# Second net last, with two sets of x buffers, and the stationary operand of the down products at the far end of the on-chip memory

## The chip, the cores and the metric

The kernel runs on one core of a Trainium2 chip. The metric is the time of one execution on the device in microseconds (us); the median of several runs counts. The core has TensorE (PE in the profile; its weight loads are PEld), VectorE (DVE), ScalarE (ACT), GpSimd (POOL) and SyncE (SP), whose queue issues all DMA transfers of this kernel. The on-chip memory has 128 partitions; sums of matmuls are made in PSUM banks and copied out by DVE or ACT.

## The reference

Three stages follow each other: an attention within chunks of 64 rows, a mixture of eight experts whose gate is normalised over rows and columns in turn, and a second net.

```python
attn = softmax(scale * q_c @ k_c.T)            # 4 batches x 8 heads x 9 chunks of 64, head_dim 64
x = (attn @ v_c) as [2304, 512]
P = exp(x @ w_gate - max)                      # [2304, 8]
for _ in range(8): P normalised by rows, then by columns
x1 = sum over e of P[:, e] * (relu(x @ w1[e]) @ w2[e])      # w1 [8, 512, 1024], w2 [8, 1024, 512]
h = max(x1 @ v1, x1 @ v2, x1 @ v3)             # the second net: [512, 768] each
out = h @ w_out                                # [768, 512]
```

The second net's weights come in as 64-bit numbers and are decoded on the chip.

## The kernel before

**Precision.** Each operand of a large product is split into a high and a low half (`hilo`, lines 180 to 182: ACT copies the high half, DVE or POOL subtracts to get the low one). A product is then three matmuls: high by high, high by low, low by high.

**Tiling.** The 2304 rows are 18 tiles of 128 in three blocks `sb` of six. Each block's x stands in the buffers `xh` and `xl`, in the seven combinations of Strassen's scheme (four quarters and their differences). There is one set of these buffers, so a new block's x has to be put where the old one stands.

**Items.** The list `phases` (line 86) says which block goes through which net: "M" is the experts (32 items, each a pair of 128 hidden features), "m" the second net (nine items: three pairs of features by three weight matrices). Before the change the order is M of block 0, M of 1, m of 0, M of 2, m of 1, m of 2; I call these phases M0, M1, m0, M2, m1, m2. An item runs `up(n)`: seven products of six matmuls of 384 columns (line 235), numbered pos 0 to 6. ACT copies the first three sums out (`s`, line 240), DVE adds the next (`c`, line 243), and `finish` makes the activations `hh` and `hl`. The down products of the item before (`down`, line 267: six tiles of six matmuls of 512 columns in an M item, spread over three items in m) stand between the products; `hh` and `hl` are their stationary operand. After a down tile DVE adds it to `acc` (line 290 or 299).

**Work between the products.** `at(n, pos, fn)` puts a function behind product `pos` of item `n`. Every engine executes its own list in that order, and so does SP's queue.

- `decode_all` (lines 410 to 447) decodes the second net's weights: 24 jobs of eight or nine steps. A job's first DVE instruction (line 388) writes the tile `scm`. It shares its one buffer (tag `dhi`) with the job's last result `dhi`, which is stored to the DRAM array `scr` at line 447. So the next job's first step waits for that store to land. In the kernel before, all steps lie in the 30 items after M1's first one, eight steps an item.
- `x_load` (four quarters in 12 transfers), `x_sums` (four differences on DVE) and `x_put` (per product one ACT copy and one subtraction on DVE or POOL) make the next block's x in the last four items before each phase; `x_put(pos)` writes over the x of product `pos` right after its last use.
- `y_out` transposes a finished tile of the experts' output and stores it in `ys`, in the items after an M phase.
- `fetch` and `fetch2` load an item's weights (`wh`, `wl`; `w2h`, `w2l`) from DRAM on SP's queue. Every third item's `wh` and `wl` stand in a third buffer, pool `late`, at the upper end of the memory.

Of the kernel before, what the change touches and what calls it, by code (L numbers as in the profile page):

```python
# [9 lines left out]
F32 = mybir.dt.float32  # L10
F32R = mybir.dt.float32r
# [7 lines left out]
P = 128  # L19
# [10 lines left out]
KD = DM // P  # L30
SB = 3
TS = NT // SB
W = TS * P // 2
NPAIR = E * F // 256
# [3 lines left out]
NPE = 6  # L38
# [9 lines left out]
def kernel(ctx: ExitStack, tc: tile.TileContext, qk, vv, wg, wts, wts2, out):  # L48
    nc = tc.nc
    pool = lambda name, bufs=1, **kw: ctx.enter_context(tc.tile_pool(name=name, bufs=bufs, **kw))  # L50
    cp = pool("const")
    wp = pool("w", 2)
    hp_ = pool("h", 2)
    tp_ = pool("t", 1)
    raws = ExitStack()
    rp = raws.enter_context(tc.tile_pool(name="raw", bufs=1, side="right"))
# [13 lines left out]
    mr = cp.tile([1, P], F32, name="mr")  # L70
    rs = cp.tile([P, NT], F32, name="rs")
    cs = cp.tile([P, E], F32, name="cs")
    cp.tile([P, 480], F32, name="gap")
    xh = cp.tile([P, 7, 2, W], F32R, name="xh")
    xl = cp.tile([P, 7, 2, W], F32R, name="xl")
    xs = dram.tile([NT, P, KD, P], F32, name="xs")
    ys = dram.tile([NT, P, KD, P], F32, name="ys")
# [5 lines left out]
    wts2 = wts2.bitcast(I32)  # L83


    phases = [("M", 0), ("M", 1), ("m", 0), ("M", 2), ("m", 1), ("m", 2)]
    items, first_of = [], []
    for kind, sb in phases:
        first_of.append(len(items))
# [11 lines left out]
    st, sw, wh, wl, w2h, w2l = {}, {}, {}, {}, {}, {}  # L101
# [85 lines left out]
    def up(n):  # L187
        it = items[n]
        bank = {"a": ps_a.tile([P, 512], F32, name="pa", tag="pa"),
                "g": ps_g.tile([P, 512], F32, name="pg", tag="pg"),  # L190
                "b": ps_b.tile([P, 512], F32, name="pb", tag="pb")}
        bank = {k: t[:, :W] for k, t in bank.items()}
        begun = set()
        tiny = lambda nm: tp_.tile([P, W], F32, name=nm, tag=nm)
        m2 = it["kind"] == "m"
        if not m2:
            c = tp_.tile([P, 3, W], F32, name="c", tag="c")
        elif it["i"] == 0:
            mt[0] = big[0].tile([P, 4, W], F32, name="m", tag="big")
            c = mt[0]  # L200
        else:
            c = tp_.tile([P, 3, W], F32, name="c", tag="c")
        if it["down"]:
            hh = hp_.tile([P, 4, W], F32R, name="hh", tag="hh")
            hl = hp_.tile([P, 4, W], F32R, name="hl", tag="hl")
            it["h"] = (hh, hl)

        def finish(q, src):

            if not m2:  # L210
                nc.scalar.activation(out=hh[:, q], in_=src, func=AF.Relu)  # L211
                if q.start == 0:
                    nc.scalar.activation(out=src, in_=src, func=AF.Relu)  # L213
                    nc.gpsimd.tensor_tensor(out=hl[:, q], in0=src, in1=hh[:, q].bitcast(F32),  # L214
                                            op=ALU.subtract)
                    return
                nc.vector.scalar_tensor_tensor(out=hl[:, q], in0=src, scalar=0.0,  # L217
                                               in1=hh[:, q].bitcast(F32), op0=ALU.max, op1=ALU.subtract)
                return
            m = mt[0]  # L220
            if it["i"] == 0:
                if q.start == 3:
                    nc.scalar.copy(out=m[:, q], in_=src)
                return
            nc.vector.tensor_tensor(out=m[:, q], in0=src, in1=m[:, q], op=ALU.max)
            if it["i"] == 2:
                hilo(hh[:, q], hl[:, q], m[:, q])

        s = {}
        for pos, (wi, xi, b) in enumerate(PRODUCTS):  # L230
            ps = bank[b]
            for k in range(2):
                ws = slice(k * P, (k + 1) * P)
                for i, (x, y) in enumerate(((wh[n], xh), (wh[n], xl), (wl[n], xh))):
                    nc.tensor.matmul(ps, lhsT=x[:, wi, ws], rhs=y[:, xi, k], start=b not in begun,  # L235
                                     stop=k == 1 and i == 2, skip_group_check=True)
                    begun.add(b)
            if pos < 3:
                s[pos] = tiny(f"s{pos}")
                nc.scalar.copy(out=s[pos], in_=ps)  # L240
            elif pos < 6:
                q, other = {3: (0, 0), 4: (1, 1), 5: (2, 2)}[pos]
                nc.vector.tensor_tensor(out=c[:, q], in0=ps, in1=s[other], op=ALU.add)  # L243
                if pos == 4:
                    finish(slice(0, 2), c[:, 0:2])
                elif pos == 5:
                    finish(slice(2, 3), c[:, 2:3])
            else:
                finish(slice(3, 4), ps.unsqueeze(1))
            yield pos  # L250
# [94 lines left out]
    def x_put(pos):  # L345
        i = PRODUCTS[pos][1]
        hilo(xh[:, i], xl[:, i], xst[i], nc.vector if pos % 2 == 0 else None)

    def x_head(j, r, eng):

        cols = slice(j * P, (j + 1) * P)
        T = ap_.tile([P, 4, 2, P], F32, name="xT", tag="xT", bufs=1)
        for o, a, b in ((T[:, 0], r[:, 1, 0:2], r[:, 0, 0:2]), (T[:, 1], r[:, 1, 2:4], T[:, 0]),
                        (T[:, 2], r[:, 1, 2:4], r[:, 1, 0:2]), (T[:, 3], r[:, 0, 2:4], T[:, 1])):
            eng.tensor_tensor(out=o, in0=a, in1=b, op=ALU.subtract)
        yield
        raw = r[:, 0].rearrange("p (i k) q -> p i k q", i=2)
        nc.scalar.copy(out=xh[:, 0:2, :, cols], in_=raw)
        nc.scalar.copy(out=xh[:, 2, :, cols], in_=r[:, 1, 2:4])
        nc.gpsimd.tensor_tensor(out=xl[:, 0:2, :, cols], in0=raw, in1=xh[:, 0:2, :, cols].bitcast(F32),  # L360
                                op=ALU.subtract)
        nc.gpsimd.tensor_tensor(out=xl[:, 2, :, cols], in0=r[:, 1, 2:4], in1=xh[:, 2, :, cols].bitcast(F32),
                                op=ALU.subtract)
        for i in range(2):
            c = slice(3 + 2 * i, 5 + 2 * i)
            nc.scalar.copy(out=xh[:, c, :, cols], in_=T[:, 2 * i:2 * i + 2])
        yield
        for i in range(2):
            c = slice(3 + 2 * i, 5 + 2 * i)
            nc.vector.tensor_tensor(out=xl[:, c, :, cols], in0=T[:, 2 * i:2 * i + 2],  # L370
                                    in1=xh[:, c, :, cols].bitcast(F32), op=ALU.subtract)
        yield


    big = [None]

    def decode_load(srcs):
        w = big[0].tile([P, 512, 2], I32, name="w64", tag="ld", bufs=3)
# [72 lines left out]
    ap_ = att.enter_context(tc.tile_pool(name="att", bufs=2))  # L451
    wones = ap_.tile([P, 2 * DM], BF16, name="wones", tag="eT", bufs=1)[:, 0:DM]
    q_t, v_t, s_t, e_t, et_t, at_t, raw_t = {}, {}, {}, {}, {}, {}, {}
# [152 lines left out]
    def at(n, pos, fn):  # L606
        bg.setdefault((n, pos), []).append(fn)

    for m in range(NT - NPE):
        t, n = NPE + m, 1 + m  # L610
# [8 lines left out]
    n = NT - NPE + 2  # L619
# [6 lines left out]

    def att_close():
        att.close()
        big[0] = pool("big")

    def raw_close():
        raws.close()
# [5 lines left out]
        for step in range(4):  # L638
            at(g + step // 3, (0, 1, 6, 1)[step], lambda g=g, step=step: keep(g, step))
    dec, folds = decode_all(), fold_all()  # L640
    for a in range(NPAIR + 1, first_of[2] - 1):
        for b in range(7):
            for _ in range(1 + (b == 3)):
                at(a, b, lambda: next(dec, None))
    at(first_of[2] - 2, 6, lambda: [None for _ in dec])
    f0 = 4 * NRAW + 2
    for i in range(NRAW * TS + 2):
        at(f0 + i // 4, (0, 2, 4, 5)[i % 4], lambda: next(folds, None))
    for k in range(1, len(phases)):
        n0 = first_of[k]  # L650
        g = x_load(k)
        for i in range(13):
            at(n0 - 4 + i // 7, i % 7, lambda g=g: next(g, None))
        for step in range(4):
            at(n0 - 2, step + 2, lambda step=step: x_sums(step))
        for pos in range(7):
            at(n0 - 1, pos, lambda pos=pos: x_put(pos))

    def warm(n):
        p = wk.tile([P, 512], F32, name="warm", tag="wk")  # L660
# [3 lines left out]
    with tc.manual_schedule():  # L664
# [14 lines left out]
        for k in range(NPE + 2):  # L679
            if k < NPE:  # L680
                att_qk(k)
                load_qk(k + 3)
            if k >= 2:
                att_pv(k - 2)
                load_v(k + 1)
            if 1 <= k <= NPE:
                att_norm(k - 1)
            if k < NPE:
                att_exp(k, 2)
            if 1 <= k <= NPE:  # L690
                att_T(k - 1)
            warm(4 if k < NPE else 0)
            if k == 0:
                prep(0, 0)
                raw1(1)
            if k == 1:
                prep(0, 1)
            if k == 3:
                prep(0, 2)
                raw2(1)  # L700
            if xg:
                next(xg.pop(0))
            if k >= 3 and k % 2:
                g = x_head(k // 2 - 1, raw_t[k // 2 - 1], nc.gpsimd if k < NPE else nc.vector)
                next(g)
                next(g)
                xg.append(g)
# [72 lines left out]
```

## Time and profile before

| | us |
|---|---|
| three runs | 1940.75, 1938.32, 1941.76 (median 1940.75) |
| the profiled execution | 1934.4 |
| its span, first to last instruction | 1932.6 |
| PE busy | 1882.9 (97%) |
| DVE, ACT, POOL busy | 1116.0, 690.7, 636.1 |
| PE's share of the chain that ended last | 88% |

Matmuls overlap each other in the records, so "busy" tells little; the start of one to the start of the next is the pace. An item's time is taken from the start of its first matmul to that of the next item's first.

### The profile page before, as it was taken

What the parts mean: (1) busy time and instruction counts of PE and PEld (TensorE: products, weight loads), DVE (VectorE), ACT (ScalarE), POOL (GpSimd) and SP (SyncE); (2) the same over time, 40 slices, a digit from 0 to 9 for tenths busy, and PEclk for the clock granted to TensorE, in tenths of its full rate; (3) what the DMA queues carried; (4) which work ended last, traced back from release to release, by engine and by line L of the source; (5) the groups of instructions that cost most, each with busy time, mean ns of one, the idle gap of its engine ahead of it and who ended that gap; (6) DMA issues with size and microseconds to landing.
All of it is one profiled execution on the core that took longest, in us unless ns stands there. A gap on an engine that the chain in (4) does not pass through costs nothing.

```text
span 1932.6 us, 26875 instructions
## 1 busy us (share of the span) xinstructions
PE 1882.9 (97%) x10397; PEld 1681.6 (87%) x10403; DVE 1116.0 (58%) x1748; ACT 690.7 (36%) x1194; POOL 636.1 (33%) x438
## 2 busy tenths in 40 slices
PE   7999999999999999999999999999999999999998
PEld 4988888888888888889888989898989988889897
DVE  7566555637875777677766545444445444453534
ACT  4545554454444333233323332322222222233221
POOL 6666666778872221222221211211111111111201
PEclk8999999999999999999999999999999999999999
DMA  7587967778888766767776457544444444647562
GB/s 252 189 301 265 329 248 278 284 278 297 328 325 300 255 228 235 269 240 253 264 264 226 188 214 259 212 180 179 180 180 180 182 189 191 225 172 253 192 247 93
DMA packets 172673, 455.30 MB, mean 236 GB/s; under 512 B 14465, under 2 KB 81025, under 8 KB 172545
## 3 DMA queue, kind: packets, MB, share of 16 engines
q1 hardware_dynamic: 172544, 453.58, 64.1%
q8 instruction: 82, 1.34, 0.3%
q14 instruction: 47, 0.38, 0.1%
HBM read 319.57 MB, written 132.38 MB: 234 GB/s over the span
## 4 chain that ended last, share of the span: by engine, by line
PE 88%; DVE 4%; DMA 4%; ACT 3%; issue 1%; POOL 1%; SPq 0%; DVEq 0%; ACTq 0%; POOLq 0%
PE dn L267 42%; PE pa L235 24%; PE pg L235 12%; PE pb L235 6%; DMA w2l<-w2s 2%; DMA scr<-dhi 1%; PE s L478 1%; PE gp L569 1%; DVE c L243 1%; PE warm L662 1%; ACT hh L211 1%; PE xp L557 1%; DVE acc L290 1%; DVE xl L182 1%; DVE hl L217 0%
## 5 line engine op out<-in xcount | busy, mean ns | idle before, releaser
L267 PE MATMUL dn<-w2h,hh 128*128 128x512 f32 x1260 | 498.9, 396 | 12.3 <-ACT hh L181 6.0
L267 PE MATMUL dn<-w2h,hl 128*128 128x512 f32 x1260 | 502.8, 399 | 3.7 <-DVE hl L217 3.4
L267 PE MATMUL dn<-w2l,hh 128*128 128x512 f32 x1260 | 499.8, 397 | 2.8 <-DMA w2l<-w2s 2.8
L290 DVE SCALAR_TENSOR_TENSOR acc<-dn,Pt,acc 128x512 f32<-128x512 f32 x438 | 327.1, 747 | 276.2 <-PE dn L267 274.8
L214 POOL TENSOR_TENSOR hl<-c,hh 128x768 fp32r<-128x768 f32 x96 | 177.9, 1853 | 828.3 <-ACT c L213 820.0
L235 PE MATMUL pa<-xh,wh 128*128 128x384 f32 x984 | 333.8, 339 | 8.0 <-ACT s L240 8.0
L235 PE MATMUL pa<-xl,wh 128*128 128x384 f32 x984 | 331.9, 337 | 0.0
L235 PE MATMUL pa<-xh,wl 128*128 128x384 f32 x984 | 330.9, 336 | 0.0
L211 ACT ACTIVATE hh<-c 128x768 fp32r<-128x768 f32 x192 | 131.8, 687 | 451.5 <-DVE c L243 451.2
L267 PEld LDWEIGHTS dn<-w2h,hl 128*128 128x128 f32 x1260 | 237.6, 189 | 59.3 <-DVE hl L217 7.0
L267 PEld LDWEIGHTS dn<-w2h,hh 128*128 128x128 f32 x1260 | 238.6, 189 | 46.4 <-ACT hh L181 6.6
L267 PEld LDWEIGHTS dn<-w2l,hh 128*128 128x128 f32 x1260 | 237.9, 189 | 33.8 <-DMA w2l<-w2s 4.0
L240 ACT COPY s<-pa 128x384 f32<-128x384 f32 x246 | 118.1, 480 | 251.7 <-PE pa L235 251.6
L235 PEld LDWEIGHTS pa<-xh,wh 128*128 128x128 f32 x984 | 185.4, 188 | 23.7 <-ACT s L240 11.1
L235 PEld LDWEIGHTS pa<-xl,wh 128*128 128x128 f32 x984 | 185.3, 188 | 13.2
L235 PEld LDWEIGHTS pa<-xh,wl 128*128 128x128 f32 x984 | 185.3, 188 | 0.0
L235 PE MATMUL pg<-xh,wh 128*128 128x384 f32 x492 | 166.7, 339 | 3.7 <-DVE c L243 3.7
L235 PE MATMUL pg<-xl,wh 128*128 128x384 f32 x492 | 167.1, 340 | 0.0
L235 PE MATMUL pg<-xh,wl 128*128 128x384 f32 x492 | 166.4, 338 | 0.0
L217 DVE SCALAR_TENSOR_TENSOR hl<-c,hh 128x384 fp32r<-128x384 f32 x96 | 109.0, 1135 | 60.6 <-ACT hh L211 59.4
L243 DVE TENSOR_TENSOR c<-pb,s 128x384 f32<-128x384 f32 x114 | 63.1, 554 | 99.2 <-PE pb L235 93.9
L240 ACT COPY s<-pg 128x384 f32<-128x384 f32 x123 | 59.1, 480 | 156.1 <-PE pg L235 155.9
(123 smaller groups left out, 2372.4 us busy)
## 6 DMA issues: line engine op xcount, KB each, us to landing
wh<-w1s SPq DMA_DIRECT2D x64, 896.0 KB, 4.7
wl<-w1s SPq DMA_DIRECT2D x64, 896.0 KB, 6.6
w2h<-w2s SPq DMA_DIRECT2D x64, 512.0 KB, 7.4
w2l<-w2s SPq DMA_DIRECT2D x64, 512.0 KB, 8.2
w1s<-wh SPq DMA_DIRECT2D x32, 896.0 KB, 7.4
w1s<-wl SPq DMA_DIRECT2D x32, 896.0 KB, 9.1
wh<-scr SPq DMA_DIRECT2D x27, 896.0 KB, 4.7
wl<-scr SPq DMA_DIRECT2D x27, 896.0 KB, 6.6
```

Source lines behind the costliest of these rows:

```text
L182: (eng or nc.gpsimd).tensor_tensor(out=l, in0=v, in1=h.bitcast(F32), op=ALU.subtract)
L211: nc.scalar.activation(out=hh[:, q], in_=src, func=AF.Relu)
L214: nc.gpsimd.tensor_tensor(out=hl[:, q], in0=src, in1=hh[:, q].bitcast(F32), op=ALU.subtract)
L217: nc.vector.scalar_tensor_tensor(out=hl[:, q], in0=src, scalar=0.0, in1=hh[:, q].bitcast(F32), op0=ALU.max, op1=ALU.subtract)
L235: nc.tensor.matmul(ps, lhsT=x[:, wi, ws], rhs=y[:, xi, k], start=b not in begun, stop=k == 1 and i == 2, skip_group_check=True)
L240: nc.scalar.copy(out=s[pos], in_=ps)
L243: nc.vector.tensor_tensor(out=c[:, q], in0=ps, in1=s[other], op=ALU.add)
L267: nc.tensor.matmul(p, lhsT=h[:, hi, ts], rhs=w[:, f, :], start=(f == 0 and i == 0), stop=(f == 1 and i == 2))
L290: nc.vector.scalar_tensor_tensor(out=acc[t], in0=p, scalar=Pt[:, t, e:e + 1], in1=acc[t], op0=ALU.mult, op1=ALU.add)
L478: nc.tensor.matmul(ss[g][cs, hp, :], lhsT=a[r, hp, 0, cs], rhs=a[r, hp, 1, cs], start=True, stop=True)
L557: nc.tensor.matmul(p[64 * g:64 * g + 64, hp, :].rearrange("p (a q) -> p a q", a=2), lhsT=v[r, h * D:(h + 1) * D], rhs=aT[r, :, he, :], sta ...
L569: nc.tensor.matmul(p, lhsT=x[:, k, :], rhs=wgr[:, k, :], start=k == 0, stop=k == KD - 1)
```

## The change

- `phases` becomes M0, M1, M2, m0, m1, m2.
- The decoding spreads over the items of M1 and M2: one step behind every second product (3.5 an item) instead of eight an item in M1 alone.
- x of M1, M2 and m0 is still made by `x_load`, `x_sums` and `x_put`. For m1 and m2 a new `x_next` does it, from the second item of the phase before on: per two tiles it loads whole tiles of `ys`, takes four differences on DVE, casts on ACT, and subtracts on POOL and DVE. `x_head`, which did this at the start for the first block, becomes `x_cols`. For m1 it writes a second set `xbh`, `xbl`; for m2 again `xh`, `xl`, which m1 doesn't use.
- `big_again` closes the pool of decoding buffers after M2 and opens a new one that holds `xbh` and `xbl`.
- The pool of `hh` and `hl` moves from the lower side to the upper end of the memory, above `late`. Small unused tiles (`gap`, `edge`) set the starts: x, weights and `hh`, `hl` began 352 bytes past a multiple of 512 and `late` 480 past one; now all of them begin at a multiple of 512.

```diff
-    hp_ = pool("h", 2)
+    pool("edge", side="right").tile([P, 120], F32, name="edge")
+    hp_ = pool("h", 2, side="right")
...
-    cp.tile([P, 480], F32, name="gap")
+    cp.tile([P, 8], F32, name="gap")
...
-    phases = [("M", 0), ("M", 1), ("m", 0), ("M", 2), ("m", 1), ("m", 2)]
+    phases = [("M", 0), ("M", 1), ("M", 2), ("m", 0), ("m", 1), ("m", 2)]
...
+        vh, vl = xb if first_of[4] <= n < first_of[5] else (xh, xl)
...
-                for i, (x, y) in enumerate(((wh[n], xh), (wh[n], xl), (wl[n], xh))):
+                for i, (x, y) in enumerate(((wh[n], vh), (wh[n], vl), (wl[n], vh))):
...
+    def x_next(k):
+
+        for j in range(TS // 2):
+            r = big[0].tile([P, 2, KD, P], F32, name="xr", tag="xr")
+            for q in range(2):
+                nc.sync.dma_start(out=r[:, q], in_=ys[phases[k][1] * TS + 2 * j + q])
+            yield
+            yield
+            yield
+            yield from x_cols(j, r, nc.vector, big[0], *(xb if k == 4 else (xh, xl)))
...
-    for a in range(NPAIR + 1, first_of[2] - 1):
-        for b in range(7):
-            for _ in range(1 + (b == 3)):
-                at(a, b, lambda: next(dec, None))
-    at(first_of[2] - 2, 6, lambda: [None for _ in dec])
+    for a in range(NPAIR + 1, first_of[3] - 1):
+        for b in range(a % 2, 7, 2):
+            at(a, b, lambda: next(dec, None))
+    at(first_of[3] - 2, 6, lambda: [None for _ in dec])
...
-    for k in range(1, len(phases)):
+    for k in range(1, 4):
...
+    at(first_of[3] - 1, 6, big_again)
+    for k in (4, 5):
+        g = x_next(k)
+        for a in range(first_of[k - 1] + 1, first_of[k]):
+            for b in range(0, 7, 2):
+                at(a, b, lambda g=g: next(g, None))
```

The first place is DVE's list in M1, where one decoding job ends and the next begins. `V` is the job's decoded block (its last DVE rows are the differences), `scm` the next job's first tile, `acc` the sum of down tiles. Before:

```order
L125 TENSOR_TENSOR V<-V 128x128
L290 SCALAR_TENSOR_TENSOR acc<-dn,Pt,acc 128x512
L388 TENSOR_SCALAR scm<-w_7443 128x512
L290 SCALAR_TENSOR_TENSOR acc<-dn,Pt,acc 128x512
L392 TENSOR_SCALAR scm<-scm 128x512
```

After, at the same job's end:

```order
L126 TENSOR_TENSOR V<-V 128x128
L292 SCALAR_TENSOR_TENSOR acc<-dn,Pt,acc 128x512
L219 SCALAR_TENSOR_TENSOR hl<-pa,hh 128x384
L292 SCALAR_TENSOR_TENSOR acc<-dn,Pt,acc 128x512 x2
L409 TENSOR_SCALAR scm<-w_8702 128x512
L292 SCALAR_TENSOR_TENSOR acc<-dn,Pt,acc 128x512
```

Between the block's last difference and the first row of the next job stood one sum of a down tile; now three sums and a low half stand there.

The second place is ACT's list at the end of m1, in its last item and the first copies of m2; `xh<-xf` is the cast of `x_put`, `m` the running maximum of the second net. Before:

```order
L181 CAST xh<-xf_15784 128x768
L181 CAST xh<-xf_15781 128x768
L181 CAST hh<-m 128x768
L181 CAST xh<-xf_15785 128x768
L181 CAST hh<-m 128x384
L181 CAST xh<-xf_15782 128x768
L181 CAST hh<-m 128x384
L181 CAST xh<-xf_15786 128x768
L240 COPY s_16149<-pa 128x384
```

After, the same item and, in the second fence, where x of m2 is made now, in the sixth item of m1:

```order
L182 CAST hh<-m 128x768
L182 CAST hh<-m 128x384 x2
L242 COPY s_15659<-pa 128x384
```

```order
L242 COPY s_15840<-pa 128x384
L362 CAST xh<-xr 128x4x128
L363 CAST xh<-xr 128x2x128
L370 CAST xh<-xT 128x4x128 x2
L242 COPY s_15854<-pg 128x384
```

The casts of x left the last item of the phase, where they stood between the casts of `hh`, and stand in groups of four in earlier items.

## Rows read from the trace of the kernel before

**Rows 1.** Section 1 of the page: busy time of TensorE.

```profile
PE 1882.9 (97%) x10397; PEld 1681.6 (87%) x10403; DVE 1116.0 (58%) x1748; ACT 690.7 (36%) x1194; POOL 636.1 (33%) x438
```

**Rows 2.** Stretches: start:end, length, PE, PEld, DVE, ACT, POOL (instructions), clock, DMA, GB/s.

```profile
585.87:605.15 19.28, 18.22 (x100) 15.93 (x99) 11.64 (x17) 8.15 (x15) 3.70 (x2) 1.00 0.79 297
605.15:1110.80 505.65, 494.24 (x2425) 438.69 (x2423) 342.18 (x602) 167.82 (x277) 108.30 (x57) 0.99 0.69 246
1110.80:1208.48 97.68, 94.68 (x511) 88.46 (x511) 46.13 (x66) 30.00 (x57) 13.17 (x9) 1.00 0.64 234
1208.48:1231.21 22.73, 18.76 (x80) 16.09 (x80) 11.95 (x15) 6.82 (x12) 8.15 (x5) 0.85 0.50 184
1231.21:1716.65 485.44, 485.44 (x2420) 436.56 (x2419) 239.26 (x340) 136.09 (x227) 61.15 (x33) 1.00 0.50 189
1716.65:1816.06 99.41, 96.40 (x512) 90.00 (x512) 45.77 (x66) 30.02 (x57) 13.15 (x9) 0.98 0.63 230
1816.06:1833.23 17.17, 13.10 (x55) 11.59 (x55) 8.91 (x11) 4.50 (x9) 6.27 (x4) 0.80 0.34 130
1833.23:1906.23 73.00, 71.38 (x380) 67.09 (x380) 28.53 (x43) 18.17 (x36) 7.62 (x6) 1.00 0.56 211
...
1843.40:1853.49 10.09, 10.09 (x56) 9.56 (x55) 4.94 (x9) 2.28 (x4) 0.64 (x1) 1.00 0.89 337
1853.49:1864.66 11.17, 10.36 (x55) 9.50 (x55) 3.75 (x5) 3.39 (x7) 3.17 (x3) 1.00 0.51 183
1246.85:1262.49 15.64, 15.64 (x80) 14.06 (x79) 7.18 (x11) 4.16 (x7) 1.85 (x1) 1.00 0.49 185
1262.49:1278.19 15.70, 15.70 (x80) 14.13 (x79) 7.73 (x12) 4.15 (x7) 1.85 (x1) 1.00 0.49 185
```

**Rows 3.** What TensorE waited for in M1: total us, times, longest.

```profile
PE dn L267 <- DMA w2h<-w2s: 3.7, 2, 2.4
PE dn L267 <- DVE hl L217: 3.4, 5, 1.0
PE dn L267 <- DMA w2l<-w2s: 2.8, 4, 0.7
```

**Rows 4.** DVE's groups in M1: busy us, mean ns | idle before, and its releasers.

```profile
L388 DVE TENSOR_SCALAR scm<-w 128x512 int32<-128x512 int32 x24 | 11.7, 488 | 65.2 <-DMA scr<-dhi 40.9 <-issue 8.3 <-DMA w<-in_wts 7.4
```

**Rows 5.** Timeline of M1, all engines, where one decoding job follows another: start, us.

```profile
771.40 0.28 DVE L125 TENSOR_TENSOR V<-V 128x128 f32<-128x128 f32 x1
...
771.72 0.94 ACT L181 CAST dhi<-V 128x896 fp32r<-128x896 f32 x1 [1.11 <-DVE V L125]
...
772.69 0.52 SPq L447 DMA_DIRECT2D scr<-dhi  x1
...
776.00 0.43 DVE L388 TENSOR_SCALAR scm<-w 128x512 int32<-128x512 int32 x1 [3.65 <-issue]
```

**Rows 6.** Timeline from m1's end into m2's first item, all engines.

```profile
1816.10 0.83 ACT L181 CAST xh<-xf 128x768 fp32r<-128x768 f32 x1
...
1816.96 2.02 DVE L182 TENSOR_TENSOR xl<-xf,xh 128x768 fp32r<-128x768 f32 x1 [1.64 <-ACT xh L181]
...
1819.51 0.54 DVE L243 TENSOR_TENSOR c<-pg,s 128x384 f32<-128x384 f32 x1
...
1820.10 0.56 PE L235 MATMUL pg<-xh,wh 128*128 128x384 f32 x1 [2.84 <-DVE c L243]
```

**Rows 7.** The tile xT of `x_head` at the start: ns, shortest/median/longest.

```profile
L366 ACT CAST xh<-xT x6: 617/618/618, 26.3 to 44.1; 128x512 fp32r<-128x512 f32 x6
L370 DVE TENSOR_TENSOR xl<-xT,xh x6: 1211/1222/1752, 26.9 to 45.1; 128x512 fp32r<-128x512 f32 x6
...
L355 DVE TENSOR_TENSOR xT<-xr x2: 427/958/1489, 40.9 to 41.7; 128x256 f32<-128x256 f32 x2
```

**Rows 8.** Timeline of PE at the tail, down products alone: start, us; 14 matmuls between.

```profile
1925.01 0.39 PE L267 MATMUL dn<-w2l,hh 128*128 128x512 f32 x1
...
1928.41 0.39 PE L267 MATMUL dn<-w2l,hh 128*128 128x512 f32 x1
```

More of the change, by code (lines that the diff above doesn't have):

```diff
@@ L347, in x_put, with x_cols @@
         hilo(xh[:, i], xl[:, i], xst[i], nc.vector if pos % 2 == 0 else None)
-    def x_head(j, r, eng):
+    xb = []
+    def x_cols(j, r, eng, pl, xh, xl):
         cols = slice(j * P, (j + 1) * P)
-        T = ap_.tile([P, 4, 2, P], F32, name="xT", tag="xT", bufs=1)
+        T = pl.tile([P, 4, 2, P], F32, name="xT", tag="xT", bufs=1)
         for o, a, b in ((T[:, 0], r[:, 1, 0:2], r[:, 0, 0:2]), (T[:, 1], r[:, 1, 2:4], T[:, 0]),
@@ L372, in x_head, with big_again @@
         yield
-    big = [None]
+    def x_next(k):
[7 more added lines that the diff above has]
+            yield from x_cols(j, r, nc.vector, big[0], *(xb if k == 4 else (xh, xl)))
+    def big_again():
+        bigs.close()
+        big[0] = ctx.enter_context(tc.tile_pool(name="big2", bufs=1))
+        big[0].tile([P, 4, W], F32, name="m", tag="big")
+        xb.extend(big[0].tile([P, 7, 2, W], F32R, name=nm) for nm in ("xbh", "xbl"))
+    big, bigs = [None], ExitStack()
     def decode_load(srcs):
@@ L628, in att_close @@
         att.close()
-        big[0] = pool("big")
+        big[0] = bigs.enter_context(tc.tile_pool(name="big", bufs=1))
     def raw_close():
@@ L703 @@
             if k >= 3 and k % 2:
-                g = x_head(k // 2 - 1, raw_t[k // 2 - 1], nc.gpsimd if k < NPE else nc.vector)
+                g = x_cols(k // 2 - 1, raw_t[k // 2 - 1], nc.gpsimd if k < NPE else nc.vector, ap_, xh, xl)
                 next(g)
```

## The prediction

> **What bounds the kernel now.** I read the page's first section, then stretches cut at the phases, then waits, then single places in the timeline. TensorE is busy 97% [rows 1], so the question is where its matmuls run at full pace and where they wait. Stretches cut at item starts tell that [rows 2]: an item of M2 takes 15.64 us with TensorE busy for all of it, and the 31 items after M2's first take 485.44, or 15.66 each. The same 31 items of M1 take 505.65. The difference, 20.2 us, is what the decoding does to TensorE, since nothing else differs between the two stretches but for the transpose of one finished tile. The second kind of loss is each phase's first item: 22.73 us in M2 and 17.17 in m2, at a mean clock of 0.85 and 0.80, against 15.64 and 10.09 for plain items [rows 2]. So some 7 us are lost at each of these two: the wait, and behind it a spell at TensorE's lower clock level (1.2 instead of 2.4 GHz). The change works on both kinds of loss. What it can't touch is the pace itself, unless the new addresses do.
>
> The waits in M1 have two roots [rows 3]. One is the down weights coming late (6.5 us together): they stand in SP's queue behind the decoding's stores, which wait for ACT and POOL. The other is the low half `hl` coming late from DVE (3.4 us). DVE is late because the first step of a decoding job sat idle 65.2 us in its 24 times, 40.9 of them until the store `scr<-dhi` had landed [rows 4]. One such place [rows 5]: the block's last difference starts at 771.40 on DVE, ACT casts it from 771.72 to 772.66, the store is issued at 772.69, and the next job's first instruction starts at 776.00 after 3.65 us of idling. The store takes some 3.3 us to land, and DVE had only one sum to do in that time. All that is queued behind the waiting instruction (sums of down tiles, `c`, `hl`) is late, and TensorE waits for `hl`.
>
> **The change, part by part.** The sum goes by phases in the order of time; M0 (585.87 us) stays as it is.
>
> *Decoding over two phases.* The steps cost the same DVE, ACT and POOL time as before, in twice as many items, beside TensorE. What changes is the spacing. A store now has two products and two down tiles between the cast and the instruction that waits for it, where it had one. Seven products and six down tiles make 15.64 us, so two such pairs are about 4.5 us; cast, issue and landing took 4.3 (771.72 to 776.00) [rows 5]. The wait shrinks to about nothing. The DVE cause goes with it, and SP's queue is free at the time of `fetch2` in most items, since only one item in 2.6 has a store at all. By its place in the order a store still stands shortly ahead of `fetch2` (behind product 0 or 1) six times, and its successor's first step ahead of the next `c` (behind 3 or 4) nine times. For these I leave 2 us in M1 and 2 in M2 of the 20.2. Bounds: 0, and the whole 20.2 if each job goes on to cost what it cost. M1 after: 19.28 + 485.4 + 2 = 506.7, which is 18.2 less.
>
> *M2 behind M1.* Its first item now stands where M1's first stood, behind an M phase: 19.28 us [rows 2], plus 1.5 for decoding steps among the casts of `x_put` (bounds 0 and 3.5, by which the worst first item of an M phase, 22.73, lies above 19.28). Then 485.44 + 2. Together 508.2, against 22.73 + 485.44 = 508.17 before: no change. The 7 us that M2's first item saves pay for the transposes of M1's finished tiles, which m0 paid before, and for the decoding.
>
> *m0 behind M2.* It is made as m0 and m1 were, behind an M phase and with `x_put`: 97.68 and 99.41 [rows 2], so 98.5, which is 0.8 more.
>
> *m1 and m2 without `x_put`.* At m2's start [rows 6] ACT casts x at 1816.10, DVE's subtraction for it takes from 1816.96 to 1818.98, the sum `c` behind it comes at 1819.51 instead, and TensorE gets its bank only then: 2.84 us of waiting, and the lower clock after it. With x made earlier, this item is like any that begins a new pair of features: 11.17 us [rows 2], 6.0 less than 17.17. m1 becomes such a first item, seven items as in m2 and a plain one: 11.2 + 73.0 + 10.1 = 94.3, which is 5.1 less than 99.41 (it loses its transposes to m0 as well).
>
> *The new `x_next`.* Per phase three groups: on ACT four casts of at most 0.618 us [rows 7], about 2.2 us a group; on DVE four differences of 0.43 to 1.49 (the long ones beside POOL) and two subtractions of 1.2 to 1.75, so 4 to 9.5 us a group. Over the seven plain items of m2 ACT is busy 18.17 and DVE 28.53 of 73.0 us [rows 2], so even 28 us more on DVE have room, and what `x_sums` and `x_put` did goes. A group's casts stand behind the copy that the next product waits for (the copy of pos 0, order of ACT above), and the results are needed items later. I take 0. If no cast were covered, six groups of 2.2 would cost 13 us. SP issues six whole-tile loads a phase in place of twelve quarters; their one buffer makes SP wait for POOL's last subtraction, with the weights of the item after next queued behind it, which have an item of 10.09 us to spare.
>
> *The places in memory.* The trace has one layout of `hh` and `hl`, so their price is bounded by other rows. Down products alone, at the tail, start every 3.40 / 15 = 226.7 ns [rows 8], 13.3 above 512 columns at 2.4 GHz. An item's 78 matmuls have 14.40 us of columns, and 15.64 is 15.9 ns above for each. So something in the mix of products costs up to 0.2 us an item, which a better placement could at best give back: 21 us over 96 M items and the smaller m items. On the other side, an item whose `wh` and `wl` lie at the upper end takes 15.70 [rows 2], 0.06 over 42 matmuls, or 1.4 ns each. For 3780 down products that would be 5.4 us more. I take 0: whichever of the two buffers an item uses, it takes 15.64, and that the upper end costs 0.06 is the nearest row.
>
> The Trainium skill says of this, in "TensorE: Matmul & The Clock Gate", section "Step-by-step: what each phase is for", that loading the next weights "doesn't steal SBUF read bandwidth from the running matmul". By that rule no placement could matter: the term would be 0 as taken, 1912 us in all, and the two rivals of placement below would have no chance. By the rows the sum lies between 1891 and 1917, and since the 13.3 ns and the 0.06 us above don't fit the rule well, the two keep theirs.
>
> **Sum.** M1 −18.2, M2 0, m0 +0.8, m1 −5.1, m2 −6.0: −28.5 us against the profiled 1934.4 (span 1932.6 and 1.8 around it), so 1905.9. The median of the runs shown, 1940.75, stands 6.35 above that execution; the same loss taken from it gives **1912 us**.
>
> **The rivals.**
> - *The decoding costs the same per job* (the change doesn't do what it says: fewer steps an item, as many stalls). For it: SP's queue still issues each store ahead of some `fetch2`. Against it: the 4.5 against 4.3 us above. The 18.2 shrinks to about 2: 1929 us. Chance 0.11.
> - *The upper end costs the down products what it costs the others*: 1912 + 5.4, about 1917. For it: 15.70 against 15.64. Against it: `late` also began 128 bytes off the others modulo 512, and that goes. Chance 0.15.
> - *The placement gives the surcharge back*: 1912 − 21 = 1891. For it: the tail's 226.7 ns. Against it: the tail runs at that pace from the old addresses, so the mix makes it, not the place. Chance 0.08.
> - *Slower: the waits on the store move to the worst place.* In the new order nine jobs have their first step behind product 3 or 4, just ahead of the sums that `hh` and `hl` are made from. M2, which had no stall, gets half of them. If the stores land late there, each could cost what the worst first item lost by a wait and the lower clock after it, some 7 us (22.73 against 15.64): 9 × 7 = 63 us against the 28.5, so 1975. It decides from 3.2 us for each of the nine. Against it: DVE idled 65.2 / 24 = 2.7 us a job at the closer spacing. Chance 0.04.
>
> **How the numbers follow.** The forecast has 0.62, with its own range 1905 to 1921 (0 to 10 us of decoding stalls left, 97.7 to 99.4 in m0, 0 to 3.5 in M2's first item). The range 1896 to 1930 takes in the upper end's cost and the decoding rival, and part of a gain by placement; it leaves out most of 0.08, the 0.04 and some of the tails. A measurement tells 0.2%, some 3.9 us, from no change. Of the slower side there is the last rival and a little of `x_next` fully exposed together with the decoding rival; no change (1937 to 1945) is the same two in part. Faster 0.92, same 0.03, slower 0.05.
>
> **What would show it.** In the profile after: M1's items after the first in about 487 us in place of 505.65; the idle time before the decoding's first step (line 409 now) far under 65.2; M2 about 508; m1 and m2 beginning with items near 11.2 us at full clock; plain items at 15.64. A plain item off 15.64 by more than 0.05 says that the placement counts, and its sign which way. I am wrong if M2 shows stalls of several us, or if casts of `xbh` stand ahead of a copy for which TensorE waits.

## The result, and the profile after

The changed kernel takes **1914.27 us** (median of four runs, 1913.18 to 1916.24), against 1939.70 for the kernel before beside it (1938.32 to 1941.76): a ratio of 0.9869, 95% interval 0.9852 to 0.9886. 1912 had been forecast. The profiled execution of after took 1915.35, with a span of 1913.6.

The first section of its page, which answers to [rows 1]:

```profile
PE 1874.1 (98%) x10397; PEld 1674.3 (87%) x10403; DVE 1125.6 (59%) x1768; ACT 689.9 (36%) x1204; POOL 638.7 (33%) x444
```

Stretches of after, cut as in [rows 2] and with the same columns (start:end, length, PE, PEld, DVE, ACT, POOL, clock, DMA share, GB/s): first item and rest of M1, first item and rest of M2, m0, m1's first item, all of m1, m2's first item, m2 with the tail; then two plain items of M2, one with its weights in `late`:

```profile
588.19:607.50 19.31, 18.25 (x99) 15.90 (x99) 11.64 (x17) 8.15 (x15) 3.70 (x2) 1.00 0.79 297
607.50:1100.59 493.09, 488.44 (x2425) 435.54 (x2424) 292.79 (x474) 151.04 (x252) 82.41 (x44) 1.00 0.61 220
1100.59:1122.88 22.29, 19.82 (x99) 17.30 (x99) 15.44 (x21) 9.06 (x16) 7.57 (x4) 0.92 0.69 230
1122.88:1611.62 488.74, 486.81 (x2426) 435.94 (x2424) 290.18 (x462) 151.42 (x253) 83.73 (x45) 1.00 0.60 218
1611.62:1709.05 97.43, 94.50 (x511) 88.26 (x511) 51.57 (x81) 32.52 (x65) 16.96 (x14) 1.00 0.62 235
1709.05:1720.22 11.17, 10.36 (x55) 9.52 (x55) 5.13 (x7) 2.22 (x5) 3.15 (x3) 1.00 0.52 199
1709.05:1802.95 93.90, 91.48 (x487) 85.77 (x487) 49.81 (x76) 27.90 (x57) 18.51 (x16) 1.00 0.66 244
1802.95:1814.12 11.17, 10.36 (x55) 9.52 (x55) 5.13 (x7) 2.22 (x5) 3.15 (x3) 1.00 0.53 199
1802.95:1913.60 110.65, 102.00 (x523) 93.37 (x522) 44.78 (x65) 23.69 (x47) 14.55 (x12) 0.98 0.46 174
1154.71:1170.35 15.64, 15.64 (x79) 14.06 (x79) 9.32 (x16) 4.69 (x8) 1.85 (x1) 1.00 0.49 186
1170.35:1185.99 15.64, 15.64 (x79) 14.06 (x79) 10.30 (x19) 4.16 (x7) 1.85 (x1) 1.00 0.48 184
```

Set against [rows 2], phase by phase, in the two profiled executions:

| | before | after | change | forecast |
|---|---|---|---|---|
| M1 | 19.28 + 505.65 | 19.31 + 493.09 | −12.5 | −18.2 |
| M2 | 22.73 + 485.44 | 22.29 + 488.74 | +2.9 | 0 |
| m0 | 97.68 | 97.43 | −0.3 | +0.8 |
| m1 | 99.41 | 93.90 | −5.5 | −5.1 |
| m2 and tail | 116.54 (1816.06 to 1932.6) | 110.65 | −5.9 | −6.0 |
| sum | | | −21.3 | −28.5 |

M1 starts 2.3 us later in the execution of after (588.19 for 585.87), so the spans differ by 19.0. The first item of M0 starts that much later too (47.38 for 45.16); over all profiles of this document it starts between 44.9 and 48.8. The medians differ by more, 25.4: the profiled execution of before (1934.4) lies 5.3 below the median of the runs beside it, that of after 1.1 above. The phases are the place to look: **7 us of the forecast are missing, all of it where the decoding runs** (5.7 in M1, 2.9 in M2, less a little that m0 and m1 gave).

What TensorE still waits for in M1 and M2 together (total us, times, longest), to be held against [rows 3], which is M1 alone:

```profile
PE dn L269 <- DVE hl L219: 4.4, 4, 1.2
PE dn L269 <- ACT hh L213: 3.5, 2, 2.5
PE pa L237 <- DVE c L245: 1.9, 3, 0.8
PE dn L269 <- DMA w2l<-w2s: 0.2, 1, 0.2
```

The late down weights of [rows 3] are gone (6.5 us there, 0.2 here). The late `hl` is not. Its root is still the decoding's first step, which [rows 4] showed idle for 65.2 us; DVE's group in the same view of after:

```profile
L409 DVE TENSOR_SCALAR scm<-w 128x512 int32<-128x512 int32 x24 | 11.6, 485 | 45.9 <-DMA scr<-dhi 37.0 <-DMA scro<-dhi 4.3 <-POOL dlo L183 2.6
```

45.9 us of the idle time are left, 37.0 of them until the store `scr<-dhi` has landed, and 24.5 of these 37.0 in four places. There four pairs of neighbouring items are long; two plain items would take 31.28 us:

```profile
653.02:686.85 33.83, 32.06 (x157) 27.89 (x156) 18.88 (x33) 9.45 (x16) 5.79 (x4) 1.00 0.62 214
969.55:1002.99 33.44, 31.96 (x157) 27.85 (x156) 18.75 (x33) 9.45 (x16) 5.68 (x4) 1.00 0.62 216
1049.91:1083.38 33.47, 32.28 (x159) 28.18 (x158) 21.70 (x36) 9.45 (x16) 6.12 (x4) 1.00 0.64 228
1294.45:1328.61 34.16, 32.32 (x159) 28.13 (x158) 18.90 (x32) 9.67 (x17) 6.04 (x4) 1.00 0.61 212
```

Three lie in M1 and make 6.9 of the 7.7 us by which 493.09 exceeds 485.44; the fourth makes 2.9 of the 3.3 in M2. The first pair tells why. SP's queue there (start, us the issue takes), and behind it DVE's row from the same place:

```profile
654.99 0.32 SPq L171 DMA_DIRECT2D wh<-w1s  x1
655.41 0.38 SPq L171 DMA_DIRECT2D wl<-w1s  x1
655.83 0.43 SPq L179 DMA_DIRECT2D w2h<-w2s  x1
656.31 0.66 SPq L179 DMA_DIRECT2D w2l<-w2s  x1
657.56 0.62 SPq L468 DMA_DIRECT2D scr<-dhi  x1
```

```profile
667.71 0.43 DVE L409 TENSOR_SCALAR scm<-w 128x512 int32<-128x512 int32 x1 [6.92 <-DMA scr<-dhi]
```

The transfers issued in these microseconds (the last number is us from issue to landing), and then the same store as the median of its 18 issues in M1 and M2:

```profile
w2l<-w2s SPq DMA_DIRECT2D x1, 512.0 KB, 9.6
scr<-dhi SPq DMA_DIRECT2D x1, 448.0 KB, 10.1
```

```profile
scr<-dhi SPq DMA_DIRECT2D x18, 448.0 KB, 3.2
```

The store is issued right behind the four loads of a whole item's weights and lands 10.1 us after its issue, 1.7 us after the last of them (657.56 + 10.1 against 656.31 + 9.6). The median is 3.2, near the 3.3 of [rows 5]. In all four long pairs the store stands directly behind such loads (in the third one load of a quarter of x lies between), and it lands after 10.1, 9.7, 8.1 and 10.1 us. Two stores that are issued 3.7 us after the last of such loads, in place of 1.2, land after 6.4; the first steps that waited for them idled 2.3 us each, and that cost TensorE next to nothing (the items behind took 15.90 and 15.87 for 15.64). The Trainium skill says in "DMA: Bandwidth & Descriptors", section "Queues, rings and completion order", that a queue's descriptors are consumed in ring order on each DMA engine. These landings agree with it.

The remaining excess is M2's first item, 22.29 us at a clock of 0.92. Its rows, all engines:

```profile
1094.30 0.28 DVE L123 TENSOR_TENSOR V<-V 128x128 f32<-128x128 f32 x1
1094.41 1.89 POOL L183 TENSOR_TENSOR xl<-xf,xh 128x768 fp32r<-128x768 f32 x1 [2.64 <-ACT xh L182]
...
1094.62 1.82 DVE L124 TENSOR_TENSOR V<-V 128x128 f32<-128x128 f32 x1
...
1100.54 1.98 DVE L183 TENSOR_TENSOR xl<-xf,xh 128x768 fp32r<-128x768 f32 x1 [2.57 <-ACT xh L182]
...
1103.11 0.54 DVE L245 TENSOR_TENSOR c<-pg,s 128x384 f32<-128x384 f32 x1
...
1104.26 0.50 PE L269 MATMUL dn<-w2h,hh 128*128 128x512 f32 x1 [2.47 <-ACT hh L213]
...
1106.04 0.52 PE L237 MATMUL pg<-xh,wh 128*128 128x384 f32 x1
...
1106.36 0.52 PE L237 MATMUL pg<-xl,wh 128*128 128x384 f32 x1
```

A decoding subtraction of 128 columns takes 1.82 us on DVE beside POOL's subtraction for `x_put` (the one ahead of it took 0.28), ACT and DVE then run late through the rest of `x_put`, `c` comes at 1103.11 and `hh` behind it, and TensorE waits 2.47 us. Some 1.5 us after the wait its matmuls of 384 columns start 0.32 us apart (1106.04, 1106.36), which is 384 columns at 1.2 GHz, the lower level; that lasts until about 1109.

### The profile page after: what moved, and what is told of

Read it like the earlier page. It is cut to its first block, busy times and chain, and to the rows that moved or that the text cites. A ratio compares the mean times of both kernels' runs of the same rounds, so it can differ in the third digit from the quotient of the medians.

```text
span 1913.6 us, 26868 instructions
## 1 busy us (share of the span) xinstructions
PE 1874.1 (98%) x10397; PEld 1674.3 (87%) x10403; DVE 1125.6 (59%) x1768; ACT 689.9 (36%) x1204; POOL 638.7 (33%) x444
## 4 chain that ended last, share of the span: by engine, by line
PE 90%; DMA 3%; DVE 3%; ACT 2%; POOL 1%; issue 1%; SPq 0%; ACTq 0%; DVEq 0%; POOLq 0%
PE dn L269 43%; PE pa L237 25%; PE pg L237 13%; PE pb L237 6%; DMA scr<-dhi 2%; DMA w2l<-w2s 1%; PE s L499 1%; PE gp L590 1%; PE warm L688 1%; PE xp L578 1%; ACT hh L213 1%; DVE c L245 1%; DVE acc L292 0%; PE yp L310 0%; DVE hl L219 0%
## 5 line engine op out<-in xcount | busy, mean ns | idle before, releaser
L237 PE MATMUL pa<-xh,wh 128*128 128x384 f32 x912 | 307.8, 338 | 6.8 <-ACT s L242 4.9
L237 PE MATMUL pa<-xl,wh 128*128 128x384 f32 x912 | 306.7, 336 | 0.0
L237 PE MATMUL pa<-xh,wl 128*128 128x384 f32 x912 | 305.2, 335 | 0.0
L237 PEld LDWEIGHTS pa<-xh,wh 128*128 128x128 f32 x912 | 171.5, 188 | 22.7 <-ACT s L242 6.8
L237 PEld LDWEIGHTS pa<-xl,wh 128*128 128x128 f32 x912 | 171.3, 188 | 13.3
L237 PEld LDWEIGHTS pa<-xh,wl 128*128 128x128 f32 x912 | 171.2, 188 | 0.0
L237 PE MATMUL pg<-xl,wh 128*128 128x384 f32 x456 | 154.0, 338 | 0.0
L237 PE MATMUL pg<-xh,wh 128*128 128x384 f32 x456 | 152.9, 335 | 0.4 <-DVE c L245 0.4
L237 PE MATMUL pg<-xh,wl 128*128 128x384 f32 x456 | 153.1, 336 | 0.0
```

## The experiments

The theory at this point: the wait of the shared buffer `dhi` on the store, not the number of decoding steps in an item, makes the loss in M1 and M2; making the x of m1 and m2 early carries most of the gain; the addresses matter little. The rivals: the steps themselves cost TensorE by their number, so that only spacing helps; the late down weights make the loss; the places in memory carry a part of the gain. None of the kernels below leaves out any of the computation.

**The kernel again**, as the measure for the rest.

> The changed kernel as it is, on the same chip as the next three: 1914 us, phases M1 512.4, M2 511.0, m0 97.4, m1 93.9, m2 about 107.

Measured: 1914.36 us (1912.85 to 1917.18), the kernel before beside it 1936.13, ratio 0.9890 (0.9877 to 0.9904). M1 took 512.80 and M2 511.71, within 0.7 us of the first profile. m2 with the tail took 109.03, not the 107 expected, and 1.6 less than the 110.65 of the first profile, in which the mean clock there was 0.98:

```profile
1802.04:1911.07 109.03, 100.38 (x523) 92.21 (x522) 44.78 (x65) 23.70 (x47) 14.56 (x12) 1.00 0.47 176
```

The kernel before came out at 1936 to 1937 beside all the experiments, not at 1940.

**`hh` and `hl` back below, old start residues.** After with

```diff
-    pool("edge", side="right").tile([P, 120], F32, name="edge")
-    hp_ = pool("h", 2, side="right")
+    hp_ = pool("h", 2)
...
-    cp.tile([P, 8], F32, name="gap")
+    cp.tile([P, 96], F32, name="gap")
```

> The changed kernel with the pool of hh and hl back on the lower side and the old residues (x, weights, hh, hl 352 bytes past a multiple of 512, late 480 past one). My theory: the placement is worth next to nothing. Plain items 15.64 us, those with weights in late 15.70 again, all phases within 2 us of the changed kernel's (M1 512.4, M2 511.0, m0 97.4, m1 93.9, m2 110.7). Rival: the placement carries a share of the gain; then plain items go above 15.64 or the phases grow by 5 us or more together.

Measured: 1918.03 (one run). An item with weights in `late` and the plain one behind it:

```profile
815.72:831.42 15.70, 15.70 (x79) 14.14 (x79) 9.51 (x18) 4.99 (x8) 3.98 (x2) 1.00 0.77 277
831.42:847.06 15.64, 15.64 (x79) 14.06 (x79) 9.32 (x16) 4.69 (x8) 1.86 (x1) 1.00 0.48 184
```

The 0.06 us of `late` items is back; where `hh` and `hl` lie changes nothing for the others. Each phase lies within 0.7 us of after's, as expected, and all of them together are 1.2 us longer (one execution of each kernel).

**`hh` and `hl` below, all starts at multiples of 512**:

```diff
-    hp_ = pool("h", 2, side="right")
+    hp_ = pool("h", 2)
```

> The changed kernel with the pool of hh and hl back on the lower side, but all buffers still starting at multiples of 512. If the 15.70 us of items with weights in late came from the upper end itself, those items take 15.70 here; if it came from the residue (late began 128 bytes off the others modulo 512), they take 15.64 here and 15.70 only in e1. My theory: the residue, 15.64.

Measured: 1916.26 (one run). The same `late` item:

```profile
816.20:831.84 15.64, 15.64 (x80) 14.06 (x79) 9.51 (x18) 5.00 (x8) 3.97 (x2) 1.00 0.77 278
```

`late` is at the upper end in both kernels. So the 0.06 came from its start, 480 bytes past a multiple of 512 where the rest stood at 352, not from the end of the memory at which it lies. Whether the 480 itself or the difference of 128 counts was not tried.

**Decoding in M1 alone again**, the rest as in after:

```diff
-    for a in range(NPAIR + 1, first_of[3] - 1):
-        for b in range(a % 2, 7, 2):
-            at(a, b, lambda: next(dec, None))
-    at(first_of[3] - 2, 6, lambda: [None for _ in dec])
+    for a in range(NPAIR + 1, first_of[2] - 1):
+        for b in range(7):
+            for _ in range(1 + (b == 3)):
+                at(a, b, lambda: next(dec, None))
+    at(first_of[2] - 2, 6, lambda: [None for _ in dec])
```

> The changed kernel with the decoding put back into M1 alone, eight steps an item. My theory (the spacing of the steps took the stalls away): M1's items after the first go from 493.1 back to about 505 us, M2's from 488.7 to 485.4, M2's first item from 22.3 to about 19.3; in sum 6 us slower than the changed kernel, some 1920. Rival (the stalls went for another reason, the order of phases or the placement): M1 stays near 493 and the kernel gets faster by M2's 3 to 6 us, about 1909.

Measured: 1917.68 (1917.14 to 1918.56), ratio 0.9901 (0.9882 to 0.9920). M1 behind its first item, and M2's first:

```profile
608.75:1110.38 501.63, 492.28 (x2426) 436.61 (x2424) 342.32 (x602) 167.84 (x277) 108.23 (x57) 1.00 0.69 248
1110.38:1129.61 19.23, 18.25 (x100) 15.88 (x99) 11.56 (x17) 8.16 (x15) 3.69 (x2) 1.00 0.55 203
```

M1 went back to 501.63 only, not to the 505 expected. Spreading saves 8.5 us there (501.63 to 493.09) and gives 3.1 back in M2's first item and 3.3 in its rest (485.4 here). The net is 2.1 us by these phases and 3.3 by the medians of two groups of runs (1917.68 and 1914.36), hardly clear of their scatter. The forecast had counted 14.7: 18.2 less the 3.5 that it put into M2.

**x of m1 and m2 by `x_load`, `x_sums` and `x_put` again**, in one set of buffers:

```diff
-        vh, vl = xb if first_of[4] <= n < first_of[5] else (xh, xl)
+        vh, vl = xh, xl
...
-        xb.extend(big[0].tile([P, 7, 2, W], F32R, name=nm) for nm in ("xbh", "xbl"))
...
-    for k in range(1, 4):
+    for k in range(1, 6):
...
-    for k in (4, 5):
-        g = x_next(k)
-        for a in range(first_of[k - 1] + 1, first_of[k]):
-            for b in range(0, 7, 2):
-                at(a, b, lambda g=g: next(g, None))
```

> The changed kernel without x_next: x of m1 and m2 is made by x_load, x_sums and x_put in the last items of the phase before, in one set of buffers. My theory: the first items of m1 and m2 go from 11.2 back to about 17.2 us each with the lower clock behind the wait; 12 us slower, about 1926. Rival (x_next itself costs what it saves, or the order alone saved it): first items stay below 13 us and the time within 4 us of the changed kernel.

Measured: 1927.07 (1926.62 to 1928.55), ratio 0.9951 (0.9934 to 0.9969). The first items of m1 and m2, 11.17 each in after:

```profile
1710.78:1728.17 17.39, 12.89 (x55) 11.31 (x55) 8.90 (x11) 4.50 (x9) 6.26 (x4) 0.80 0.33 128
1810.91:1827.78 16.87, 12.93 (x55) 11.48 (x55) 8.92 (x11) 4.50 (x9) 6.28 (x4) 0.80 0.35 132
```

The two items give 6.2 and 5.7 of the 12.8 us by which this kernel is slower than after (1927.07 against 1914.27). `x_next` is the largest part of the gain.

**A buffer of its own for `scm`.** If the wait on the shared buffer makes the loss, this takes it away whatever the spacing:

```diff
-        scm = big[0].tile([P, 2, 512], I32, name="scm", tag="dhi")
+        scm = big[0].tile([P, 2, 512], I32, name="scm", tag="scm")
```

> The changed kernel with a buffer of its own for the decoding's first tile scm, so that a job's first step no longer waits for the store of the last job's dhi. My theory (what is left of stalls in M1 and M2 comes from DVE waiting for stores that queue behind the weight loads): idle time before line 409 falls from 45.9 us to under 10, M1's items after the first take about 486 in place of 493.1, M2's about 485.5 in place of 488.7; some 10 us faster than the changed kernel, 1904. Rival (the down weights that come late, or the work of the steps itself): the same idle time goes but M1 and M2 keep their stalls, within 3 us of 1914.

Measured: 1904.82 (1903.31 to 1905.69), ratio 0.9838 (0.9825 to 0.9852). DVE's group, and M1 behind its first item, M2's first item and M2's rest:

```profile
L409 DVE TENSOR_SCALAR scm<-w 128x512 int32<-128x512 int32 x24 | 16.5, 688 | 0.0
```

```profile
604.99:1090.68 485.69, 485.66 (x2425) 436.23 (x2424) 293.92 (x474) 151.78 (x252) 82.51 (x44) 1.00 0.62 224
```

```profile
1090.68:1112.94 22.26, 19.79 (x100) 17.21 (x99) 15.24 (x21) 8.89 (x15) 7.60 (x4) 0.92 0.69 230
1112.94:1599.18 486.24, 486.01 (x2426) 436.25 (x2424) 290.98 (x463) 151.69 (x253) 83.78 (x45) 1.00 0.60 219
```

The idle time is 0.0, TensorE no longer waits for `hl` or `c` in M1 and M2, and both rests are within 0.8 us of the 485.44 of [rows 2]. One name is worth 9.5 us (1914.36 to 1904.82). M2's first item stays as it was, so that loss has another cause.

**No decoding beside `x_put` at the edge from M1 to M2**: the buffer as above, no steps in M1's last two items, four of them made up for in items of M2.

> As the one before, and no decoding step in the last two items of M1, where x_put makes x for M2 (their steps go to four items of M2). My theory (the steps between the sums of that item make M2's first item 22.3 instead of 19.3): M2's first item 19.3 at full clock, 3 us faster than e5_own_scm, about 1901. Rival (the wait there is x_put's own behind an M phase with decoding): stays at 22.

```diff
-            at(a, b, lambda: next(dec, None))
+            if a not in (first_of[2] - 2, first_of[2] - 1):
+                at(a, b, lambda: next(dec, None))
+    for a in (72, 76, 80, 84):
+        at(a, 3, lambda: next(dec, None))
```

Measured: 1901.32 (1897.66 to 1903.44), ratio 0.9819 (0.9805 to 0.9833), the fastest version. M2's first item:

```profile
1094.11:1113.36 19.25, 18.27 (x100) 15.93 (x99) 13.01 (x20) 8.69 (x16) 3.70 (x2) 1.00 0.55 203
```

19.25 at full clock for 22.26 at 0.92: decoding beside `x_put` made the 3 us. That it did so by the long subtraction of 1.82 us is read from the trace; no run takes away that one alone.

**Decoding in M1 alone, with the buffer of its own**: does the spacing matter at all without the shared buffer? The edit is the two diffs of the dense decoding and of the own buffer together.

> The dense decoding of e3_decode_dense (eight steps an item, in M1 alone) with a buffer of its own for scm. If the shared buffer is what made the decoding dear, M1's items after the first fall from 501.6 to 490 or less and the time to about 1906, and the spacing of the steps was only a way round it. If the late down weights or the work itself make the stalls, M1 stays above 497.

Measured: 1907.70 (1905.77 to 1908.94), ratio 0.9853 (0.9840 to 0.9867). M1 behind its first item:

```profile
606.60:1098.99 492.39, 487.22 (x2425) 436.36 (x2424) 362.80 (x602) 168.35 (x277) 108.78 (x57) 1.00 0.70 252
```

It misses the 490 that was expected at most, by 2.4 us. The shared buffer made 9.2 (501.63 to 492.39) of dense decoding's 16.2 us over 485.44. The other 7.0 lie in four items (17.11, 18.25, 16.47 and 17.73 for 15.64), which are the items where TensorE waits for `w2h` and `w2l`:

```profile
PE dn L269 <- DMA w2l<-w2s: 2.6, 4, 0.7
PE dn L269 <- DMA w2h<-w2s: 2.4, 2, 1.5
```

That part is what spreading cures: with an own buffer, spread against dense, M1 behind its first item takes 6.7 us less (485.69), but M2 takes 3.9 more (508.50 against 504.62), above all in its first item. By the medians spreading is then worth 2.9 us (1904.82 against 1907.70).

**Order alone and placement alone.** The first is after with the edits of the dense decoding and of `x_put` together; the second is the kernel before with the new `edge`, `gap` and side of `h` and nothing else:

```diff
-    hp_ = pool("h", 2)
+    pool("edge", side="right").tile([P, 120], F32, name="edge")
+    hp_ = pool("h", 2, side="right")
...
-    cp.tile([P, 480], F32, name="gap")
+    cp.tile([P, 8], F32, name="gap")
```

> The changed kernel with both the dense decoding of e3_decode_dense and the x_put of e4_x_put_again: what is left of the change is the order of phases and the placement. My theory (parts add up): 1927.1 + 1917.7 - 1914.3 = 1930.5, with first items of 13.3, 17.4 and 16.9 us in m0, m1 and m2 and 19.2 in M2, against 13.4, 14.9, 17.2 and 22.7 before; some 6 us faster than the kernel before. Rival (the order alone gives nothing, the parts hang on each other): 1936.

> The kernel before with the new placement alone (hh and hl at the upper end, everything at multiples of 512). My theory: items with weights in late go from 15.70 to 15.64, 2 us in all; within 3 us of the kernel before, and M1's items after the first stay between 501 and 506. Rival: the placement takes 4 us or more of M1's stalls away (M1 was 501.6 in e3_decode_dense against 505.65 before, at the same density of steps); then 1930 or less.

Measured: order and placement 1930.14 (1928.98 to 1932.05), ratio 0.9964 (0.9951 to 0.9977); placement alone 1931.33 (1925.64 to 1935.12, 11 runs), ratio 0.9969 (0.9957 to 0.9981); the kernel before 1937.04 (16 runs). The starts of m1 with the new order, and of M2 and m1 with placement alone:

```profile
1710.81:1729.08 18.27, 14.33 (x56) 12.65 (x56) 8.92 (x11) 4.50 (x9) 6.27 (x4) 0.72 0.32 122
```

```profile
1208.68:1231.49 22.81, 18.84 (x80) 16.10 (x79) 11.94 (x15) 6.82 (x12) 8.15 (x5) 0.85 0.50 184
1231.49:1716.33 484.84, 484.84 (x2420) 436.05 (x2419) 239.28 (x340) 136.12 (x227) 61.22 (x33) 1.00 0.49 189
1716.33:1729.64 13.31, 11.45 (x64) 10.22 (x63) 8.00 (x12) 4.34 (x9) 1.82 (x1) 1.00 0.41 158
```

The order by itself buys nothing that can be told (1.2 us, overlapping intervals): it mends M2's start (19.21 with it) and spoils m1's, which now follows an m phase. The 1930.5 expected as the sum of the parts came in, but nearly all of the gain over the kernel before is the placement's. The order pays only through `x_next`, whose second set of buffers stands in the memory of the decoding.

The placement is worth 5.7 us by the medians, where at most 3 had been expected; M1 behind its first item takes 503.95, as expected. In the two profiled executions the phases are 4.8 us shorter with it: 1.7 in M1, 0.5 in M2 (484.84 for 485.44 in its rest, the `late` items), 0.8 in m2 and 1.9 in m1, which is a spell at the lower clock that one of them has and the other hasn't. (The spans differ by 2.9 only, since M0 began 1.9 later, at 47.06 for 45.16.) In the new order the old places cost 1.2 us over all phases, as said above. So only one or two us are seen in item after item, and what makes the rest of the 5.7 isn't shown.

## Why the prediction was right, and where it wasn't

In medians the path from before to after is 1937.04, with the placement 1931.33, with the order 1930.14, with `x_next` 1917.68, with the spreading 1914.36 (from three groups of runs, in which the kernel before had 1936.13 to 1937.04). Against it the terms of the forecast, put in the same order:

| | forecast | runs |
|---|---|---|
| placement | 0 | −5.7 |
| order and `x_next` | −13.8 (−3.5 in M2's first item, +0.8, −5.1, −6.0) | −13.7 |
| spreading | −14.7 (−18.2 + 3.5) | −3.3 |
| sum | −28.5 | −22.7 |

**The number was 2 us off, but two errors stand against each other in it.** Spreading was forecast 11 us too good, placement 6 too bad, and the median from which the 28.5 were taken (1940.75) lies 3.7 above that of the 16 later runs of before. That median stood on three runs, and the executions of before scatter over 10 us (1931.21 to 1941.94 in all batches, beside 1934.4 in the profile): the 6.35 us between profile and median that the sum took in were partly that scatter, and gave back some of what was missing. That the number came out so close is luck.

- *m1 and m2 without `x_put`*: right in place and size. Both first items take 11.17 at full clock as [rows 2] had them; the phases gained 5.5 and 5.9 for 5.1 and 6.0.
- *`x_next` at nothing*: right. m2 behind its first item, with the tail, takes 110.65 − 11.17 = 99.48 us, for 116.54 − 17.17 = 99.37 before; m1 behind its first item takes 82.73, in after as in the kernel with `x_put` again (82.74).
- *m0*: 97.43, 0.3 below the forecast's 97.7 to 99.4.
- *The decoding*: the step that failed is "The wait shrinks to about nothing". Its time from cast to landing was taken from one place [rows 5] where the store had the queue to itself, and the count of bad places looked at stores *ahead* of an item's loads. The bad places are the stores *behind* them: these land after 8.1 to 10.1 us, and the two products and two down tiles that the new spacing puts in between are over in 4.5. Of the idle time on that store, 40.9 us in [rows 4], 37.0 stayed. The terms "2 us in M1 and 2 in M2" measured 7.7 and 3.3. The late down weights, the other part of the loss, went as forecast.
- *M2's first item*: 20.8 forecast, 22.29 measured, within its bound of 22.73. The 1.5 for decoding beside `x_put` was about the wait (2.47 us, where M1's first item has one of 1.1); the lower clock behind it came on top.
- *Placement*: plain items stayed at 15.64, so neither rival of placement happened as described: the upper end costs nothing, and the surcharge on each matmul stayed. The `late` items gained 0.06 us by their start, as the argument against the first of these rivals had it. On the Trainium skill's sentence in "TensorE: Matmul & The Clock Gate", section "Step-by-step: what each phase is for", that weight loads take no read bandwidth from the running matmul: the 15.70 and 15.64 of the two kernels with `hh` and `hl` below, which differ only in the starts of the tiles, show that an address can cost TensorE time; by what path isn't shown.
- *The rival that the decoding costs the same per job* came half true: 11.0 of the 20.2 us stayed. But they don't stay in each job; 9.8 of them sit at the four bad places, and the other twenty jobs cost next to nothing. *The slower rival* didn't come: none of the decoding's waits cost 7 us, and the four long pairs lost 2.2 to 2.9.

What stays open is where most of the placement's 5.7 us come from.

## What to carry to other kernels

Before spreading work out to cover a wait, look at what makes it wait: here two tiles shared a buffer, and a name of its own for one of them gave 9.5 us, where twice the spacing gave 2 to 3. A transfer's landing time is that of its place in the queue; take it from the worst place that it will have, behind the largest loads, not from a clean one. Making an operand early in spare buffers, items before the phase that reads it, gave back the whole start-up loss of m1 and m2 here, and the new order was worth only what such buffers got from it.

## What the runs showed of the hardware

- The same 448 KB store lands 3.2 us after its issue (median of 18), but after 8.1 to 10.1 in the four places where loads of an item's weights stand right ahead of it on the queue.
- A DVE subtraction of two operands of 128 columns took 1.82 us beside a POOL subtraction of 1.89 us that began 0.21 us earlier, and ended 0.14 us after it; the like instruction ahead of it took 0.28. The Trainium skill says in "SBUF — State Buffer", section "Who interferes with whom", that a DVE instruction with two inputs from the on-chip memory contends with a GpSimd one that reads it; these rows agree.
- An item whose weights start 480 bytes past a multiple of 512, beside others at 352, takes 15.70 us for 15.64.
- A wait of TensorE of 2.47 us at M2's start was followed by about 3 us at 1.2 GHz. Such spells differ between executions of one kernel: m2 with the tail took 110.65 us at a mean granted clock of 0.98 in one profile of after, and 109.03 at 1.00 in the other.
